# Attention with a relative bias and a three-way maxout layer: reordering the first batches' loads, sums and left-over scores

## The chip, the cores and the metric

The kernel runs on one core of one Trainium2 chip. A core has TensorE (PE in the profile; its weight loads are shown as PEld), VectorE (DVE), ScalarE (ACT), GpSimd (POOL) and SyncE (SP). DMA transfers are issued from the queues of SP, ACT and POOL. The metric is the device time of one execution in microseconds, lower is better. Chances and verdicts are about the median of several executions.

## What is computed

Eight batches of attention with eight heads of 64 columns over 576 positions, and on its result a layer that takes the maximum of three products and multiplies it by a fourth matrix. The reference, cut to what matters:

```python
scores = scale * np.matmul(q, k.transpose(0, 1, 3, 2))      # batch 8, heads 8, seq 576, head_dim 64
bucket = np.where(is_small, n, large)                       # n = abs(row - column)
scores = scores + bias_table[bucket].transpose(2, 0, 1)[None, :, :, :]
attn = np.exp(scores)                                       # after the row maximum is taken off
attn = attn / (np.sum(attn, axis=-1, keepdims=True) + 1e-09)
x = np.matmul(attn, v)                                      # then laid out as 4608 x 512
h = np.maximum(np.maximum(x @ w1, x @ w2), x @ w3)          # 512 x 768 each
out = h @ w_out                                             # 768 x 512
```

## The kernel before

**Tiling.** Batches are counted b = 0 to 7 here, as in the code; the words "batch one" and "batch two" in the change's name are b = 0 and b = 1. Heads go in pairs, hp = 0 to 3. The 576 positions are four tiles of 128 and a left-over of 64. Scores are made transposed (keys on partitions, queries along the free dimension), so that the sums over keys are matmuls with the exponentials as weights. The bias becomes a factor: exponentials near the diagonal are multiplied on VectorE by `hank`, a table of exp(bias), which is what `times_band`, `bands`, `times_bandt` and `times_band_left` do.

**A pair's work.** `visit(qT, kT, e4, c)` (L554) makes the scores of one half of the queries (256) against the four key tiles, as two PSUM tiles `sc` of two banks each, and ScalarE turns each into exponentials in `e4`. `left_keys` (L573) makes the scores of the 64 left-over keys (`sct`), `left_queries` or the optional start of `visit` (L556) those of the 64 left-over queries (`scq`); both write `el`. `attend(b, hp, e4, el, half)` (L604) makes the weighted sums with `v` (`vx` for the four tiles, `vt` for the left-over keys) of one half, in a PSUM tile `a`, and hands back `quotients`, which divides on VectorE. Sums are put off by one pair in the list `late`, and `next_late` (L670) takes the next.

**PSUM.** Three pools of two tiles each: `ps_s` (`sc`, `sct`, the `tp` of b = 1, and `scq` where `left_queries` makes it), `ps_a` (sums, `scq` where `visit` makes it, and a product's first factor while `idle_sums` is not empty), `ps_f` (products `ps`, outputs `pso`, the small transposes). A tile is given out again only when the engine that reads it is done.

**The first batch** (b = 0) has two passes over the pairs, since its inputs arrive piecewise. The first pass visits the first half of the queries; the second (L758 to L810) visits the second half, makes the left-over scores and the sums of half 0, and ends with parts of the first product block. `bands(hp)` multiplies the first half's exponentials.

**Later batches** (L813 to L894) visit both halves of a pair in turn. `together` (L818) says whether the left-over queries are made in `visit` and the half-1 sums follow the left-over keys; it is true from the second pair of b = 2 on. Between the visits `fill(target, hooks)` (L439) puts in portions of the maxout layer up to the target (`rate`) in a count where a product's first, second or third factor counts 4 and an output 6. Hooks run ahead of the last factor or output put in; with three or more of these, a first hook of two runs one place earlier. `add_ffn` cuts a block of tokens into portions; the first 512 tokens come as two blocks of 256 columns (`per` = 2), so that a factor is eight matmuls of 256 columns.

**Queues.** Each engine works in program order. q, k and v are cast to bf16 during their loads, all issued by POOL. The loads of v for b = 0 come between those of q's rest and w_bf[0]; behind them in POOL's queue are b = 1's q and k, the other weights and later batches. SP issues the crossbar transposes of b = 2 and later (L464), those of the attention's result (L651), and the stores. For b = 1 q and k are transposed on TensorE: `second_transposes` (L507), copied out of PSUM by VectorE (`qT`) and ScalarE (`kT`); `spread_packed` (L210) rearranges its loads before that.

The loop's order in b = 1, per pair: visit 0, half-0 sums of the pair before, band 0, quotients, spread of the next pair's q and k, fill with `keys`, visit 1, half-1 sums, band 1, quotients, transposes of the next pair, fill with band 2, left-over queries and band 3.

Of the kernel before, what the change touches and what calls it, by code (L numbers as in the profile page):

```python
# [39 lines left out]
def kernel(  # L40
# [12 lines left out]
    nc = tc.nc  # L53
    B, H, S, D = q.shape
# [78 lines left out]
    def in_turn(b, load):  # L133
        return inorder(load)
# [48 lines left out]
    def load_v(b, h0, h1, behind=None):  # L183
        loads = load_main(v, b, h0, h1, vx[b % 2][:, :, :, 0:D])
        go_behind(loads + load_tail(v, b, h0, h1, v_diag), behind)
# [77 lines left out]
    load_tail(k, 0, 0, H, k_diag)  # L263
    load_main(q, 0, 0, H, batch[0][0], 2, KT)
    load_q_tail(0)
    load_v(0, 0, H)

    def cast_keys(hp):
        h = slice(2 * hp, 2 * hp + 2)
# [38 lines left out]
    def make_bandt():  # L308
        for par in range(2):
            r = slice(64 * par, 64 * par + 64)  # L310
            c = BAND // 2 - 64 * par
            dve_copy(bandt[r, :, :], hank[r, par::2, c : c + 192][:, :, ::-1])
# [4 lines left out]
    def ffn(t0, nt, last):  # L317
# [79 lines left out]
        if per == 1:  # L397
            portions = [[f[0], m[0]]]
            for fb in range(1, n_fb):
                portions.append([g[fb - 1], f[fb], m[fb]])  # L400
            portions.append([g[-1], (0, None), o[0]])
        else:
            if not t0:
                portions = [[f[0]], [m[0], f[1]], [m[1]], [f[2], m[2]]]
                deferred.append(([[g[0]], g[1:]], [[x] for x in o]))
                o = []
            else:
                portions = [x for gs, _ in deferred for x in gs]
                for fb in range(n_fb):
                    portions += [[f[fb], m[fb]], [g[fb]]]  # L410
                portions += [x for _, os in deferred for x in os] + [[o[0]]]
                o = o[1:]
        if len(o) > 2:
# [256 lines left out]
    def next_late():  # L670
        return late.pop(0)() if late else (lambda: None)
# [43 lines left out]
    def bands(hp):  # L715
        for t in range(KT):
            times_band(hp, first_e[hp], t, 0, QS, inorder)
# [40 lines left out]
    for hp in range(HP):  # L758
        qT, kT = (x[:, hp, :] for x in qk[0])
        e4, el = e_tiles()  # L760
        visit(qT, kT, e4, 1, (lambda: more_transposes(hp + 1)) if hp + 1 < HP else None)
        if hp == 0:
            bands(HP - 2)
            bands(HP - 1)

        def keys():
            left_keys(hp, qT, kT, el, QS, S)

        def queries():
            left_queries(hp, qT, kT, el)  # L770

        def late_bands():
            for t in range(KT):
                times_band(hp, e4, t, QS, QM, inorder)

        if hp == 0:
            keys()
            queries()
        if hp == 1:
            x_transposes(0, 0)  # L780
        quotients = next_late()
        if hp < 2:
            quotients()
            if hp == 1:
                keys()
                queries()
                x_transposes(1, 0)
            quotients = next_late()
            quotients()
            if hp == 0:  # L790
                make_bandt()
            late_bands()
            products(hp, el)
        else:
            keys()
            quotients()
            queries()
            late_bands()
            if hp == 2:
                x_transposes(2, 0)  # L800
                x_transposes(3, 0)
                add_ffn(0, QS)
                fill(8)
            else:
                batch[2] = load_tiles()
                load_qk(2)
                x_transposes(0, 1)
                fill(8, lambda: second_transposes(qk[1], 0))
            products(hp, el)
        late.append(lambda hp=hp, e4=e4, el=el: attend(0, hp, e4, el, 1))  # L810

    turned = [lambda hp=hp: x_transposes(hp, 1) for hp in range(1, HP)]
    for b, hp in [(b, hp) for b in range(1, B) for hp in range(HP)]:  # L813
# [1 line left out]
            x_sb[b] = x_tile()  # L815
        qT, kT = (x[:, hp, :] for x in qk[b])
        e4, el = e_tiles()
        together = b > 1 and (b, hp) != (2, 0)  # L818
        rate = 8 if b == 1 or (b, hp) == (2, 0) else 13


# [21 lines left out]

        def keys():
            left_keys(hp, qT, kT, el, 0, S)
            if together:
                next_late()()

        fill(rate, keys, *([lambda: None] if together else []))
        times_bandt(hp, el)  # L850


        visit(qT, kT, e4, 1, el=el if together else None)
        store_outputs()
        if b == 1 or hp in (1, 2) and b + 1 < B:
            next(crossbar, None)
        early()
        if turned:
            turned.pop(0)()
        if not together:  # L860
            quotients = next_late()
            times_band(hp, e4, 1, 0, QM, inorder)
            quotients()
        if b == 1 and hp + 1 < HP:
            second_transposes(qk[1], hp + 1)
        if hp == 1 and b > 1:
            add_ffn((b - 1) * CH, CH)
        if hp == (2, 2, 0)[min(b, 3) - 1] and b + 1 < B:
# [8 lines left out]
            load_qk(b + 2, turned_qk[b + 1, 1, KT - 1])  # L877

        def queries():
            if not together:  # L880
                left_queries(hp, qT, kT, el)
            times_band(hp, e4, 3, 0, QM, inorder)

        def bands_2():
            for t in range(1 if together else 2, 3):
                times_band(hp, e4, t, 0, QM, inorder)

        if together:
            idle_sums.append(hp)
        fill(rate, bands_2, queries)  # L890
        idle_sums.clear()
        times_band_left(hp, el)
        for half in range(2):
# [45 lines left out]
```

The softmax here doesn't subtract the row's maximum and nothing guards it: scores larger than these inputs give would overflow.

## Time and profile before

| | us |
|---|---|
| median of 4 runs (lowest to highest) | 321.02 (320.26 to 321.56) |
| the profiled execution | 322.56 |
| its span, first to last instruction | 320.80 |

| stretch of the span | what runs | us | PE busy | DVE busy | ACT busy | granted clock |
|---|---|---|---|---|---|---|
| 0 to 16 | loads, b = 0 first pass | 16.0 | 11.94 | 8.67 | 11.17 | 1.00 |
| 16 to 36 | b = 0 second pass | 20.0 | 15.88 | 14.64 | 14.10 | 0.83 |
| 63.8 to 76.9 | b = 2, pairs 0 and 1 | 13.1 | 12.89 | 9.43 | 9.81 | 1.00 |
| 76.9 to 98 | b = 2, pairs 2 and 3, start of b = 3 | 21.1 | 19.38 | 15.34 | 14.94 | 1.00 |
| 98 to 262 | the other batches | 164.0 | 162.46 | 114.81 | 115.42 | 1.00 |
| 262 to 320.8 | rest of the maxout layer | 58.8 | 54.84 | 29.06 | 10.98 | 1.00 |

The stretch from 36 to 63.8 is b = 1. The profile is of one execution of the program. Busy times are the union of an engine's instructions in a stretch; matmuls are pipelined and their ends modelled, so a short wait between two of them can hide in a busy figure. The granted clock is the share of full clock that TensorE was given. Idle time ahead of an instruction is shown in brackets with the operation that released it. What starts a wait matters more than the share: an engine that is always busy next to one that sometimes waits sets the pace.

### The profile page before, as it was taken

The numbers are of one execution on the slowest core, as the hardware profiler recorded it, in microseconds if no ns is written. First come the engines' busy times: TensorE is split into PE (matmuls) and PEld (weight loads), VectorE is DVE, ScalarE is ACT, GpSimd is POOL, SyncE is SP. The second block draws the span as 40 slices with busy tenths as digits, with TensorE's granted clock in tenths as the row PEclk, the third lists the DMA queues.
The fourth block names the chain that finished last, engine by engine and source line by source line (L and its number), as shares of the span: only waits on it lengthen the run. The fifth ranks groups of instructions, "written<-read, shape, count | busy, mean of one in ns | idle before, by whom it ended". The sixth has DMA issues, their size and how long they took to land.

```text
span 320.8 us, 8198 instructions
## 1 busy us (share of the span) xinstructions
PE 304.6 (95%) x3288; PEld 172.1 (54%) x3328; DVE 213.6 (67%) x535; ACT 201.2 (63%) x297; POOL 108.2 (34%) x143
## 2 busy tenths in 40 slices
PE   7768899999998999999999999999999999999995
PEld 2356677775554555555555555555555554444442
DVE  6386778786675666667777677776777675554452
ACT  4958898896776667776777677767775751121221
POOL 8938831348049611950294039400000000000000
PEclk9969999999999999999999999999999999999999
DMA  9999999999999999999999959994042103301103
GB/s 167 196 197 198 182 144 135 129 110 141 181 162 155 135 210 141 125 131 181 158 140 143 190 112 153 137 187 108 2 77 98 36 2 74 133 0 67 66 0 131
DMA packets 163878, 40.34 MB, mean 126 GB/s; under 512 B 153720, under 2 KB 159360, under 8 KB 163840
## 3 DMA queue, kind: packets, MB, share of 16 engines
q0 software_dynamic: 103776, 16.66, 78.5%
q1 hardware_dynamic: 58304, 22.69, 38.3%
q10 hardware_dynamic: 1760, 0.47, 0.7%
q8 instruction: 26, 0.43, 0.6%
q14 instruction: 12, 0.10, 0.1%
HBM read 35.39 MB, written 9.45 MB: 140 GB/s over the span
## 4 chain that ended last, share of the span: by engine, by line
PE 69%; DMA 3%; SPq 1%; DVE 1%; issue 1%; ACT 1%
PE ps L94 37%; PE pso L94 13%; PE a L94 11%; PE sc L94 6%; DMA kT<-ktail 2%; PE sct L94 2%; PE scq L94 1%; SPq L464 1%; DMA out_dram<-osb 1%; DVE e L533 0%; ACT e L539 0%; DVE hT L360 0%; DVE m L354 0%; ACT osb L388 0%; SPq L389 0%
## 5 line engine op out<-in xcount | busy, mean ns | idle before, releaser
L94 PE MATMUL ps<-xT,w_bf 128*128 128x512 bf16 (+1 forms) x693 | 148.7, 357 | 2.0 <-ACT xT L107 0.6
L539 ACT ACTIVATE e<-sc 128x1024 bf16<-128x1024 f32 x128 | 124.3, 1030 | 20.5 <-PE sc L94 17.9
L94 PEld LDWEIGHTS <-w_bf 128*128 128x128 bf16 x720 | 65.4, 98 | 63.4 <-issue 5.8
L533 DVE TENSOR_TENSOR e<-e,hank 128x512 bf16<-128x512 bf16 (+2 forms) x136 | 58.6, 467 | 11.7 <-ACT e L539 9.4
L345 ACT ACTIVATE m<-ps 128x512 bf16<-128x512 f32 x48 | 29.2, 608 | 51.9 <-PE ps L94 51.9
L354 DVE TENSOR_TENSOR m<-ps,m 128x512 bf16<-128x512 f32 x48 | 33.1, 689 | 34.1 <-PE ps L94 34.0
L94 PEld LDWEIGHTS <-kT 64*128 64x128 bf16 (+1 forms) x832 | 30.0, 95 | 39.5 <-issue 25.1
L94 PE MATMUL pso<-wo_bf,hT 128*128 128x512 bf16 (+2 forms) x209 | 47.8, 373 | 0.8 <-issue 0.2
L94 PE MATMUL a<-vx,e 128*128 128x65 bf16 x1024 | 46.4, 195 | 0.0
L360 DVE TENSOR_TENSOR hT<-ps,m 128x512 bf16<-128x512 f32 x48 | 33.1, 689 | 15.9 <-PE ps L94 14.4
L94 PE MATMUL sc<-qT,kT 64*128 64x256 bf16 x512 | 41.0, 273 | 2.8 <-ACT e L539 1.8
L94 PEld LDWEIGHTS <-e 128*128 128x128 bf16 x1024 | 42.1, 99 | 0.8
L167 POOL DMA_DIRECT2D q_sb<-in_q_dram x24 | 21.9, 914 | 49.9 <-issue 18.0
L94 PE MATMUL a<-vt,el 128*128 128x130 bf16 x160 | 36.0, 225 | 1.1 <-DMA vt<-in_v_dram 1.1
L139 POOL DMA_DIRECT2D vx<-in_v_dram x32 | 28.4, 912 | 24.4 <-PE sc L94 13.2
L110 DVE COPY osb<-pso 128x512 f32<-128x512 f32 (+1 forms) x33 | 22.6, 686 | 17.9 <-PE pso L94 14.7
L641 DVE TENSOR_TENSOR x_sb<-a,rd 128x256 bf16<-128x256 f32 (+1 forms) x64 | 31.4, 491 | 2.2
L539 ACT ACTIVATE el<-scq 128x256 bf16<-128x256 f32 (+1 forms) x55 | 20.5, 416 | 19.3 <-PE scq L94 19.2
L94 PEld LDWEIGHTS <-hT 128*128 128x128 bf16 x222 | 20.1, 97 | 22.4 <-issue 1.5
L94 PEld LDWEIGHTS <-el 128*128 128x128 bf16 x416 | 24.3, 97 | 10.5 <-issue 5.7
L539 ACT ACTIVATE el<-sct 128x576 bf16<-128x576 f32 (+2 forms) x36 | 21.7, 607 | 7.1 <-PE sct L94 5.8
L167 POOL DMA_DIRECT2D k_sb<-in_k_dram x24 | 22.0, 916 | 1.3 <-DMA w_bf<-in_moe_w_dram 1.2
(71 smaller groups left out, 168.5 us busy)
## 6 DMA issues: line engine op xcount, KB each, us to landing
out_dram<-osb SPq DMA_DIRECT2D x35, 256.0 KB, 2.7
vx<-in_v_dram POOLq DMA_DIRECT2D x32, 128.0 KB, 7.5
q_sb<-in_q_dram POOLq DMA_DIRECT2D x26, 128.0 KB, 5.0
k_sb<-in_k_dram POOLq DMA_DIRECT2D x24, 128.0 KB, 5.6
w_bf<-in_moe_w_dram POOLq DMA_DIRECT2D x3, 768.0 KB, 9.8
xT<-in_k_dram SPq DMA_DIRECT2D x6, 128.0 KB, 4.4
hank<-w_dr SPq DMA_DIRECT2D x2, 384.0 KB, 6.5
wo_bf<-in_moe_w_out_dram POOLq DMA_DIRECT2D x1, 768.0 KB, 8.0
```

The source lines that it names most:

```text
L94: inorder(nc.tensor.matmul(*args, **kw))
L110: return inorder(nc.vector.tensor_copy(out_, in_))
L139: in_turn(b, nc.gpsimd.dma_start(out=dst[:, t, h0:h1, :], in_=x[:, t, h0:h1, :])) for t in range(t0, t1)
L167: loads.append(in_turn(b, nc.gpsimd.dma_start(out=dst[:, t], in_=main_part(src, b)[:, t])))
L345: nc.scalar.activation(out=st[fb]["m0"][:], in_=ps0, func=ACTF.Copy)
L354: inorder(nc.vector.tensor_tensor(out=m[:], in0=ps1, in1=st[fb]["m0"][:], op=ALU.max))
L360: inorder(nc.vector.tensor_tensor(out=block(fb), in0=ps2, in1=other, op=ALU.max))
L464: turned_qk[b, j, t] = inorder(nc.sync.dma_start_transpose(out=made[j][:, :, P * t : P * t + n], in_=src))
L533: put(nc.vector.tensor_tensor(out=e4[:, t, :, lo:hi], in0=e4[:, t, :, lo:hi], in1=hank[:, 2 * hp : 2 * hp + 2, c0:c1][:, :, ::-1], op=ALU. ...
L539: nc.scalar.activation(out=out_, in_=in_, func=ACTF.Exp, scale=inv_sqrt_d)
L641: divided[b, hp, half] = inorder(nc.vector.tensor_tensor(out=x_sb[b][:, 2 * half : 2 * half + n, P * hp : P * hp + P].rearrange("p t (h d) ...
```

## The change

For b = 0, the left-over part of v is loaded ahead of the rest, and the rest head by head (eight loads of four tiles) instead of tile by tile (four loads of eight heads). In the second pass the sums of pair 0 come before its left-over queries, the first half's bands of pair 2 go behind the first sums' quotients and those of pair 3 behind the second ones. In pair 1 the left-over keys and queries go behind the first sums' quotients.

From b = 1 on every pair works as `together` said: left-over queries at the start of the second visit, half-1 sums behind the left-over keys in the first fill, bands 1 and 2 as a hook of the second fill. `second_transposes` becomes a hook of the second fill, between bands and band 3. The portions of the second block of 256 tokens are cut as [first], [second, third] instead of [first, second], [third]. The first fill of pair 1 of b = 2 has the rate 8 instead of 13.

```diff
@@ loads of b = 0
-    load_v(0, 0, H)
+    load_tail(v, 0, 0, H, v_diag)
+    for h in range(H):
+        in_turn(0, nc.gpsimd.dma_start(out=vx[0][:, :, h, 0:D], in_=main_part(v, 0)[:, :, h, :]))
@@ ffn, second block of 256
                 for fb in range(n_fb):
-                    portions += [[f[fb], m[fb]], [g[fb]]]
+                    portions += [[f[fb]], [m[fb], g[fb]]]
@@ second pass of b = 0
         visit(qT, kT, e4, 1, (lambda: more_transposes(hp + 1)) if hp + 1 < HP else None)
-        if hp == 0:
-            bands(HP - 2)
-            bands(HP - 1)
...
         if hp == 0:
             keys()
-            queries()
         if hp == 1:
             x_transposes(0, 0)
         quotients = next_late()
         if hp < 2:
             quotients()
+            if hp == 0:
+                bands(2)
+            else:
+                keys()
+            queries()
             if hp == 1:
-                keys()
-                queries()
                 x_transposes(1, 0)
             quotients = next_late()
             quotients()
             if hp == 0:
+                bands(3)
                 make_bandt()
@@ b = 1 to 7
-        together = b > 1 and (b, hp) != (2, 0)
...
         def keys():
             left_keys(hp, qT, kT, el, 0, S)
-            if together:
-                next_late()()
-
-        fill(rate, keys, *([lambda: None] if together else []))
+            next_late()()
+
+        fill(8 if (b, hp) == (2, 1) else rate, keys, lambda: None)
         times_bandt(hp, el)
...
-        visit(qT, kT, e4, 1, el=el if together else None)
+        visit(qT, kT, e4, 1, el=el)
...
-        if not together:
-            quotients = next_late()
-            times_band(hp, e4, 1, 0, QM, inorder)
-            quotients()
-        if b == 1 and hp + 1 < HP:
-            second_transposes(qk[1], hp + 1)
...
         def queries():
-            if not together:
-                left_queries(hp, qT, kT, el)
             times_band(hp, e4, 3, 0, QM, inorder)
 
         def bands_2():
-            for t in range(1 if together else 2, 3):
+            for t in range(1, 3):
                 times_band(hp, e4, t, 0, QM, inorder)
 
-        if together:
-            idle_sums.append(hp)
-        fill(rate, bands_2, queries)
+        idle_sums.append(hp)
+        turn = [lambda: second_transposes(qk[1], hp + 1)] if b == 1 and hp + 1 < HP else []
+        fill(rate, bands_2, *turn, queries)
```

## The prediction

> **What bounds the kernel now.** I read the page first, then the stretches of the span one by one, then the order of instructions in time where the diff touches. TensorE is busy 304.6 of 320.8 us, so a change pays only where TensorE waits or runs slowly, and costs wherever it makes TensorE wait. Busy shares by stretch, with columns us, PE, PEld, DVE, ACT, POOL busy (instructions), granted clock, DMA share, GB/s:
>
> ```profile
> 4.80:8.20 3.40, 2.29 (x23) 1.15 (x23) 2.48 (x9) 1.82 (x4) 3.40 (x6) 1.00 1.66 207
> ...
> 15.00:18.40 3.40, 1.53 (x20) 0.73 (x16) 2.07 (x7) 3.35 (x6) 0.87 (x3) 1.00 1.66 220
> 18.40:21.80 3.40, 2.50 (x40) 2.35 (x40) 2.53 (x9) 0.43 (x1) 2.76 (x4) 0.51 1.20 207
> 21.80:25.20 3.40, 3.40 (x41) 2.06 (x38) 3.15 (x12) 2.56 (x4) 1.10 (x2) 0.50 1.55 191
> ```
> ```profile
> 36.00:63.80 27.80, 27.16 (x429) 20.96 (x428) 21.63 (x61) 24.73 (x38) 10.31 (x13) 1.00 1.62 145
> ```
> The opening (b = 0, second pass over the head pairs, from 14.9 us) has slack: TensorE is idle for half of 15.0 to 18.4, and runs at half clock for the next 6.8 us. The stretch of b = 1 (36.0 to 63.8) has none: TensorE 98%, and ScalarE, just behind, 89%. The order in time shows what the opening waits for, and a pair of b = 1:
>
> ```profile
> 16.99 0.30 PE L94 MATMUL sct<-qT,kT 128*128 128x320 bf16 x1 [0.80 <-ACT e L539]
> ...
> 17.90 0.29 PE L94 MATMUL scq<-qT,kT 64*128 64x64 bf16 x8 [0.62 <-ACT e L539]
> ...
> 19.30 0.29 PE L94 MATMUL a<-vt,el 128*128 128x130 bf16 x1 [1.10 <-DMA vt<-in_v_dram]
> ```
> ```profile
> 50.93 0.61 PE L94 MATMUL sc<-qT,kT 64*128 64x256 bf16 x8
> ...
> 51.41 1.94 ACT L539 ACTIVATE e<-sc 128x1024 bf16<-128x1024 f32 x2 [0.76 <-PE sc L94]
> ...
> 52.08 1.03 PE L94 MATMUL ps<-xT,w_bf 128*128 128x256 bf16 x8
> ...
> 52.95 0.41 PE L94 MATMUL sct<-qT,kT 128*128 128x512 bf16 x2
> ...
> 54.16 0.66 PE L94 MATMUL sc<-qT,kT 64*128 64x256 bf16 x8
> ...
> 54.60 1.94 ACT L539 ACTIVATE e<-sc 128x1024 bf16<-128x1024 f32 x2 [0.22 <-PE sc L94]
> ...
> 56.83 0.78 DVE L110 COPY qT<-tp 128x512 bf16<-128x512 bf16 x2
> ...
> 57.79 0.61 PE L94 MATMUL sc<-qT,kT 64*128 64x256 bf16 x8
> ```
> Pair 2 of b = 1 takes 6.86 us (50.93 to 57.79). The product at 52.08 stands between the sums and the left-over keys (sct), so the first exponential has ended before sct needs its PSUM buffer, and the second visit's exponentials start at 54.60, 3.67 us after the pair's start. One more row, at b = 3: TensorE waits 1.15 us for the transposed left-over keys, at full load otherwise:
>
> ```profile
> 97.93 0.42 PE L94 MATMUL sct<-qT,kT 128*128 128x512 bf16 x2 [1.15 <-DMA kT<-ktail]
> ```
>
> **Part 1, the opening: −2.1 us.** Now the sums of pair 0 wait for all of v, tail last (issued 11.66 to 12.95, landing 7.0 to 7.4 us later, 19.2). Changed, the two tail loads go first (1.29 us of POOL for both) and eight head loads follow. A head is 64 KB; qtail, 64 KB, took 0.69 us to issue, vx, 128 KB, 0.88. So eight take 5.5 to 7.0 us against 3.52, and w_bf[0] behind them is issued 2.0 to 3.5 us later than 12.89. It landed at 23.5 and is first read at 29.67, which covers that. Heads 0 and 1 are issued by about 11 us. Loads issued at 8.2 and 9.1 landed 4.2 us later, at 13.3 the latest; the one issued at 9.95, beside the hank loads, 8.1 later. So they land between 14.5 and 18.5; I take 15 to 16, since less is queued ahead of them. Then the sums of pair 0 start behind sct at 17.2 instead of 19.30 (bands of pair 0 end at 17.0), left-over queries follow at 17.9 as now, sums of pair 1 at 18.2, and the scores of pair 1 at 18.7 instead of 21.60.
>
> Those 2.9 us don't all last: DVE is late next. From 18.1 its queue holds quotients 0.55, bands 0.92, quotients 0.55, bands 0.92, two bandt copies 0.71, late bands 0.88, products 0.30 and the qT copy 0.32, together 5.15 (each from its row's start to the next start): 23.3. TensorE then still has 0.12 of transposes (they wait for that copy's PSUM) and 0.60 of sums before pair 2's scores: 24.0 against 26.00 now. From there both orders are the same. I take −2.1, between −0.2 (heads at 19) and −2.9.
>
> Two rules of the Trainium skill against rows. "TensorE: Matmul & The Clock Gate", section "Why this matters for your kernels", asks for no idle gap over about 3 us to keep full clock. The longest wait here is 1.10 us, and still the clock halved at 18.4: what decides is the busy share of a stretch, lost with 1.53 of 3.40 us, kept with 2.29. By the rule the changed opening can't be throttled and all of −2.1 stands. By the rows 15.0 to 18.4 gets 0.6 of sums more and about 0.2 of left-over queries (2.3, just enough), but 21.8 to 25.2 now holds the DVE wait and about 1.9 of work: if that halves the clock for 6.8 us, pairs 2 and 3 lose 1.5 and −0.6 is left. I take the rule's side for the value and the rows for the range. "DMA: Bandwidth & Descriptors", section "Anatomy of one DMA — SWDGE (gpsimd) path", prices a load at 2.0 us plus bytes over 436 GB/s: eight times 2.15 against four times 2.3, if they were serial, is 8 us later, and pair 3's heads (due at 23.5) would be missed. But four loads issued within 3.5 us were in flight together here, so only issue time counts; I take the rows.
>
> **Part 2, b = 1 and pair 0 of b = 2: +4.8 us.** Left-over queries move into the second visit, the half-1 sums into the first fill behind sct, the transposes of the next pair behind bands 1 and 2, and per first fill there is one product of eight matmuls instead of up to two. Nothing is removed but one exponential of 0.60, which becomes two (0.66). So little can be won: TensorE has 0.64 us idle in all of 36.0 to 63.8. What is lost is in the chain. Pair 2, from its first score matmul at 0:
> - first exponential 0.48 to 1.48 (51.41 and 0.97 each); sct has no product ahead of it now, waits for that PSUM buffer and starts at 1.55 (pair 1 shows it now: 43.62, sct at 45.17);
> - half-1 sums 1.80 to 2.70, product to 3.65, its copy on ScalarE 3.9 to 4.4;
> - behind it on ScalarE the two left-over exponentials, 0.55: the second visit's exponentials start at 4.95 instead of 3.67 and end at 6.9. ScalarE stood idle 0.6 to 1.0 of that, waiting for the product;
> - TensorE: left-over queries wait for the quotients (3.8), scores to 4.5, product to 5.45, then the transposes wait for the exponential at 6.0;
> - DVE: bands 1 and 2 stand ahead of the qT copy now, band 2 needs the last exponential: 7.35, the copy 0.78, and pair 3's scores start at 8.2. TensorE idles before them by 0.6.
> 8.2 against 6.86 is +1.35. The same table for the others: pair 0 +1.45 (six-wide quotients 0.70 twice and spread copies 0.93 hold the left-over queries until 4.4), pair 1 +0.85 (an xT copy of 0.36 on ScalarE in place of the product's), pair 3 +0.5 and pair 0 of b = 2 +0.8 (no transposes; second scores and next sums wait for the last exponential and band 2), pair 1 of b = 2 −0.15 (its products, 12 then 6, become 6 then 12, which covers waits of 0.41 and 0.47 at 77). Sum 4.8. The table put to the present order gives 63.4 and 94.7 for rows at 63.83 and 94.60, so I trust it to about 1 us. Bounds: +0.3 (five times 0.06 of ScalarE) and +5.5.
>
> **Part 3, the 1.15 us at 97.93: −1.2 us.** Batch 3's q and k loads wait on POOL until the last quotients of b = 1 (issued at 70.11, 4.09 after the tail before them), and SP's transposes follow. Those quotients now belong to the first fill of that pair, about 2.4 us earlier relative to TensorE, so the chain gains on TensorE by more than 1.2. POOL and SP have nothing else queued there. Bounds 0 and −1.5. The other DMA edge, batch 2's left-over keys (landing 62.3, read at 65.9), is safe while Part 2 delays TensorE.
>
> **Sum.** −2.1 + 4.8 − 1.2 = +1.5 on the profiled execution's 322.56 (span 320.80 and 1.76 around it): 324.1. The median of the runs, 321.02, lies 1.54 below that execution, so the forecast is 322.5.
>
> **Rivals.** Faster: the chain of b = 1 closes without waits because TensorE's products cover it, and only +0.3 remains: −2.1 − 1.2 + 0.3 = −3.0, 318.0. For it: ScalarE and DVE have 3 and 6 us free there, and later batches run this very order at 99%. Against: they have 12 or more 512-wide matmuls per fill to hide behind, b = 1 has 8 or 16 of 256. It is decided where Part 2 costs less than 3.3. Slower still: the heads arrive in the hank loads' shadow (the 8.1 us row) or the clock stays halved, Part 1 gives −0.2: +3.4, 324.4. Level: the three terms cancel, because Part 2 is half my size: 321.0, or the moved steps don't meet the path.
>
> **Chances.** Forecast (322.5, own range 320.6 to 324.5) 0.55; faster rival 0.22; slower still 0.15; level 0.08. About 0.3% (1 us) can be told from no change. Faster takes 0.19 of the rival and 0.02 of the forecast's tail: 0.21. Same takes level, 0.08 of the forecast and 0.03 of the rival: 0.19. Slower 0.60. The range 318.5 to 325.4 holds the forecast, the slower case and half of the faster one.
>
> **What would show it.** Sums of pair 0 at 17 to 17.5 and scores of pair 2 near 24; clock 1.00 from 18 to 32. In b = 1, sct waiting for the exponential, transposes waiting for PSUM and scores waiting for the qT copy, and 8 us from pair to pair; the wait at the later sct gone. If TensorE stays at 97% from 34 to 62 us, Part 2 is wrong and the kernel is faster.

## The result, and the profile after

The changed kernel takes 322.44 us in the median of 35 runs (321.18 to 323.98), against 321.02 for the kernel before in the same job (54 runs). The ratio is 1.0044, 95% interval 1.0032 to 1.0057: slower by 1.4 us. 322.5 was forecast. Ratios here and below are formed from fast executions, those within 1.5% of the fastest of their kernel, and are not the quotients of the medians, which count all.

| | before | after |
|---|---|---|
| profiled execution, us | 322.56 | 322.50 |
| its span, us | 320.80 | 320.70 |
| start of pair 0's left-over keys (`sct`), second pass of b = 0 | 16.99 | 18.12 |
| start of b = 1 | 36.04 | 34.37 |
| start of pair 3 of b = 2 | 86.27 | 87.52 |
| left-over keys of b = 3 | 97.93 | 97.87 |

The two profiled executions are the same length, while the medians are 1.4 us apart: the profiled execution of before was a poor one of its kind, 1.5 us above its median, and that of after is an ordinary one. Comparing the two traces alone would have said "no change". The first pass of b = 0 took 1.13 us longer in the profile of after, so its left-over keys start later although b = 1 starts earlier.

Busy time by stretch in the profile of after, with the columns us, then PE, PEld, DVE, ACT and POOL busy (instructions), granted clock, DMA share and GB/s:

```profile
15.00:18.40 3.40, 2.15 (x26) 1.20 (x23) 2.30 (x8) 3.40 (x6) 2.39 (x4) 1.00 2.06 180
18.40:21.80 3.40, 3.38 (x77) 2.59 (x74) 2.68 (x10) 2.91 (x5) 3.40 (x6) 1.00 1.17 205
21.80:25.20 3.40, 2.19 (x41) 1.48 (x41) 3.29 (x13) 2.41 (x6) 1.15 (x2) 1.00 1.57 189
...
36.00:63.80 27.80, 24.48 (x386) 19.11 (x383) 20.33 (x55) 21.59 (x38) 10.83 (x15) 1.00 1.71 149
```

The opening keeps the full clock from 15 to 25.2, where before had 0.50 for 6.8 us. From 36 to 63.8, nearly all of it b = 1, TensorE falls from 27.16 to 24.48 us busy, and ScalarE and DVE fall with it: no engine is busy nearly all the time now, they wait for each other. The order in time (start, duration, engine, line, operation, idle time before it with its releaser) shows how:

```profile
18.12 0.30 PE L94 MATMUL sct<-qT,kT 128*128 128x320 bf16 x1 [0.80 <-ACT e L541]
18.25 0.22 PE L94 MATMUL a<-vt,el 128*128 128x130 bf16 x1
...
23.89 0.32 DVE L110 COPY qT<-tp 128x320 bf16<-128x320 bf16 x1
...
24.26 0.39 PE L94 MATMUL sc<-qT,kT 64*128 64x256 bf16 x4 [0.73 <-DVE qT L110]
...
50.70 0.61 PE L94 MATMUL sc<-qT,kT 64*128 64x256 bf16 x8 [0.52 <-DVE qT L110]
...
52.25 0.41 PE L94 MATMUL sct<-qT,kT 128*128 128x512 bf16 x2 [0.24 <-ACT e L541]
...
53.39 1.04 PE L94 MATMUL ps<-xT,w_bf 128*128 128x256 bf16 x8
...
54.97 0.66 ACT L541 ACTIVATE el<-scq 128x256 bf16<-128x256 f32 x2
...
55.51 1.95 ACT L541 ACTIVATE e<-sc 128x1024 bf16<-128x1024 f32 x2
...
56.60 0.38 PE L97 MATMUL tp<-ident,q_sb 128*128 128x128 bf16 x4 [0.23 <-ACT e L541]
...
57.09 1.02 DVE L535 TENSOR_TENSOR e<-e,hank 128x768 bf16<-128x768 bf16 x2
...
58.02 0.78 DVE L110 COPY qT<-tp 128x512 bf16<-128x512 bf16 x2
...
58.76 0.61 PE L94 MATMUL sc<-qT,kT 64*128 64x256 bf16 x8 [0.57 <-DVE qT L110]
...
63.16 1.92 PE L94 MATMUL ps<-xT,w_bf 128*128 128x256 bf16 x16
...
65.56 0.39 PE L94 MATMUL sc<-qT,kT 64*128 64x256 bf16 x4 [0.16 <-ACT e L541]
...
97.87 0.41 PE L94 MATMUL sct<-qT,kT 128*128 128x512 bf16 x2
```

Sums of pair 0 now follow the left-over keys at once (18.25), and the longest wait behind them is for DVE's qT copy (24.26), as forecast. Pair 2 of b = 1 runs from 50.70 to 58.76, 8.06 us against 6.86: `sct` waits for the exponential, the second visit's exponentials start 4.81 us in instead of 3.67, the transposes 5.90 in, and the qT copy comes behind the bands. At b = 3 the wait of 1.15 us is gone.

Pair by pair from the start of b = 1 (us from each pair's first score matmul to the next pair's):

| | (1,0) | (1,1) | (1,2) | (1,3) | (2,0) | (2,1) | (2,2) | sum |
|---|---|---|---|---|---|---|---|---|
| before | 7.58 | 7.31 | 6.86 | 6.04 | 6.04 | 7.05 | 9.35 | 50.23 |
| after | 8.54 | 7.79 | 8.06 | 6.25 | 6.30 | 7.45 | 8.76 | 53.15 |
| difference | +0.96 | +0.48 | +1.20 | +0.21 | +0.26 | +0.40 | −0.59 | +2.92 |

In these two traces b = 1 starts 1.67 earlier, its pairs and those of b = 2 cost 2.92, and from the start of b = 3 to its left-over keys 3.33 becomes 2.01: −1.67 + 2.92 − 1.32 = −0.07, which is the −0.06 between the two executions. What a typical execution does needed the experiments.

### The profile page after: what moved, and what is told of

Same layout as the page of the kernel before. It is cut to its first block, busy times and chain, and to the rows that moved or that the text cites. A ratio compares the mean times of both kernels' runs of the same rounds, so it can differ in the third digit from the quotient of the medians.

```text
span 320.7 us, 8208 instructions
## 1 busy us (share of the span) xinstructions
PE 303.9 (95%) x3288; PEld 171.7 (54%) x3328; DVE 213.5 (67%) x535; ACT 201.5 (63%) x302; POOL 110.9 (35%) x147
## 4 chain that ended last, share of the span: by engine, by line
PE 79%; ACT 2%; DVE 2%; issue 2%; DMA 1%; DVEq 0%
PE ps L94 41%; PE pso L94 14%; PE a L94 13%; PE sc L94 8%; PE sct L94 2%; PE scq L94 2%; ACT e L541 2%; DVE e L535 1%; DMA out_dram<-osb 1%; DVE x_sb L643 0%; DVE hT L353 0%; DVE hT L362 0%; ACT kT L107 0%; ACT osb L390 0%; DVE k_sb L213 0%
## 5 line engine op out<-in xcount | busy, mean ns | idle before, releaser
L535 DVE TENSOR_TENSOR e<-e,hank 128x512 bf16<-128x512 bf16 (+2 forms) x136 | 59.4, 472 | 8.6 <-ACT e L541 8.4
L94 PE MATMUL a<-vx,e 128*128 128x65 bf16 x1024 | 45.0, 193 | 0.0
L94 PEld LDWEIGHTS <-e 128*128 128x128 bf16 x1024 | 40.7, 97 | 0.9
L139 POOL DMA_DIRECT2D vx<-in_v_dram x28 | 24.8, 900 | 29.0 <-PE scq L94 15.0
```

What stands on the lines that cost most here:

```text
L94: inorder(nc.tensor.matmul(*args, **kw))
L139: in_turn(b, nc.gpsimd.dma_start(out=dst[:, t, h0:h1, :], in_=x[:, t, h0:h1, :])) for t in range(t0, t1)
L535: put(nc.vector.tensor_tensor(out=e4[:, t, :, lo:hi], in0=e4[:, t, :, lo:hi], in1=hank[:, 2 * hp : 2 * hp + 2, c0:c1][:, :, ::-1], op=ALU. ...
```

## The experiments

All were timed beside the kernel before, whose median differs from job to job: 321.02 for the first four below, 320.75 for the next four, 321.17 for the next three and 320.62 for the last. So medians of different jobs can be told apart only roughly; the ratio is to the kernel before in the same job. The start of b = 1 and the time from pair 0's left-over keys to it are collected in one table behind them.

**The kernel before, once more.**

> The kernel before, unchanged, run as a kernel of its own, so that the clock of each of its executions is listed. The two profiled spans are equal (320.8 and 320.7) while the medians differ by 1.4, so the profiled execution of before is not a typical one. Theory 1: it lost more clock than most (0.989, 6.8 us at half clock behind 18.4); typical executions have 0.995 to 1.000 and a span near 319.3. Theory 2: the clock has nothing to do with it; spans vary by 1 to 2 us at equal clocks, and a second profile has its own waits in the opening. Ratio 1.000 by both.

Measured: 321.01 us (22 runs), ratio 1.0004 (0.9987 to 1.0021); profiled execution 321.95. Stretches of 2 us of this profile, columns as above:

```profile
8.00:10.00 2.00, 1.71 (x15) 0.79 (x11) 0.87 (x3) 1.89 (x2) 2.00 (x4) 1.00 2.03 180
...
18.00:20.00 2.00, 0.58 (x12) 0.35 (x11) 1.86 (x8) 2.00 (x3) 1.16 (x2) 1.00 1.19 210
20.00:22.00 2.00, 2.00 (x37) 2.00 (x35) 1.14 (x4) 0.62 (x2) 1.03 (x2) 0.50 1.24 206
```

The clock halves here too, two us later and for a shorter time than in the first profile: the second pass takes 17.21 us instead of 19.05. But this execution was slow earlier. Until about 13 us its matmuls take as long as at half clock, although the stretches give 1.00 there; four score matmuls of the first pass, here and in the first profile of before:

```profile
9.81 0.61 PE L94 MATMUL sc<-qT,kT 64*128 64x256 bf16 x4 [0.29 <-DVE kT L110]
```
```profile
8.28 0.39 PE L94 MATMUL sc<-qT,kT 64*128 64x256 bf16 x4 [0.51 <-ACT e L539]
```

So pair 0's left-over keys start at 18.83 instead of 16.99, and b = 1 starts at 36.04 in both profiles. The wait at b = 3's left-over keys is 0.54 instead of 1.15, and these 0.61 us are the whole difference of the two spans (320.18 and 320.79). Theory 1's span near 319.3 didn't come. By the start of b = 1 the first profile had lost no more than this one; only its DMA wait was longer.

**The opening alone** (loads of v and order of the second pass, nothing from b = 1 on).

```diff
-    load_v(0, 0, H)
+    load_tail(v, 0, 0, H, v_diag)
+    for h in range(H):
+        in_turn(0, nc.gpsimd.dma_start(out=vx[0][:, :, h, 0:D], in_=main_part(v, 0)[:, :, h, :]))
...
             quotients()
+            if hp == 0:
+                bands(2)
```

> Before with the opening alone changed (v's tail first, v head by head, sums ahead of left-over queries, bands of pairs 2 and 3 later). Theory 1 (a path of waits): b = 1's first scores come 2.1 to 2.8 us earlier than in a profile of before with the same clock in the first pass; ratio 0.991 to 0.995. Theory 2 (the gain is only the clock of one odd execution): ordinary executions of before don't lose clock there, and the gain is under 0.7 us, ratio 0.998 or more. If the parts add, this ratio times that of the later part alone gives 1.0044.

Measured: 320.90 us (23 runs, 319.12 to 326.67), ratio 0.9983 (0.9965 to 1.0001), hardly a gain: by this interval the opening is worth 0 to 1.1 us, by its middle 0.5. The profiled execution is a long one, 325.49. b = 1 starts at 33.18, 2.86 before the old one, but b = 2 shows a wait that the prediction did not list. POOL's row and TensorE's, in order of time:

```profile
61.56 3.52 POOL L139 DMA_DIRECT2D vx<-in_v_dram  x4 [8.15 <-PE sc L94]
...
72.43 0.27 PE L94 MATMUL a<-vt,el 128*128 128x130 bf16 x1 [4.80 <-DMA vt<-in_v_dram]
72.49 0.65 PE L94 MATMUL a<-vx,e 128*128 128x65 bf16 x8
```

The sums of (2,0) wait 4.80 us for batch 2's v. POOL issues that load behind the fourth key tile that SP has turned for b = 2, a chain of DMAs that didn't move when TensorE was earlier (61.26 in the trace of before with b = 1 at 36.04, 61.56 here with b = 1 at 33.18). And its landing is uneven: the left-over part took 6.6 to 6.9 us here, 3.1 to 3.5 in the profile of after. Behind the wait eight sums take 0.65 us instead of 0.41: the clock has gone too.

**Everything from b = 1 on, the opening left as before.**

```diff
-                    portions += [[f[fb], m[fb]], [g[fb]]]
+                    portions += [[f[fb]], [m[fb], g[fb]]]
...
-        together = b > 1 and (b, hp) != (2, 0)
...
+        turn = [lambda: second_transposes(qk[1], hp + 1)] if b == 1 and hp + 1 < HP else []
+        fill(rate, bands_2, *turn, queries)
```

> Before with everything from b = 1 on changed and the opening left alone. Theory 1 (the chain through ScalarE and VectorE): the pairs from b = 1 pair 0 to b = 2 pair 2 take 2.9 us longer together, as in the profile of the changed kernel, and the wait of 1.15 us at b = 3's left-over keys goes: +1.7, ratio 1.0055. Theory 2 (the wait doesn't go when this part stands alone, because TensorE is late by less than the loads gain): +2.9, ratio 1.009. Theory 3 (most of the 1.4 us comes from the opening): ratio below 1.002.

Measured: 322.88 us (7 runs), ratio 1.0064 (1.0039 to 1.0089): 1.9 to 2.1 us slower. This is Parts 2 and 3 of the prediction together. By the median it is more than the whole change costs, though the intervals overlap; 0.9983 for the opening times 1.0064 is 1.0047, near the 1.0044 of both, so the parts add. The pairs are those of the changed kernel (8.52, 7.79, 7.99, 6.25, 6.31, 7.44), and `sct` of b = 3 doesn't wait. The surprise is in the opening, in the old order:

```profile
17.60 0.30 PE L94 MATMUL sct<-qT,kT 128*128 128x320 bf16 x1 [0.80 <-ACT e L539]
...
18.74 0.23 PE L94 MATMUL a<-vt,el 128*128 128x130 bf16 x1
...
20.04 0.39 PE L94 MATMUL sc<-qT,kT 64*128 64x256 bf16 x4
...
23.30 0.32 DVE L110 COPY qT<-tp 128x320 bf16<-128x320 bf16 x1
...
23.67 0.39 PE L94 MATMUL sc<-qT,kT 64*128 64x256 bf16 x4
```

This execution lost no clock from 16 to 36 us. v was there when the sums of pair 0 came, pair 2's scores start 6.07 us behind pair 0's left-over keys (6.14 in the changed kernel), and b = 1 starts 16.12 behind them (16.25 in the changed one). In both, pair 2's scores come when DVE's qT copy is done (the rows at 23.30 here and 23.89 there), and it starts 5.70 and 5.77 us behind the left-over keys. At full clock the old order is as quick as the new one.

**The q and k loads of b = 3 earlier, else as before.**

```diff
-            load_qk(3, divided[1, HP - 1, 1])
+            load_qk(3, divided[1, HP - 1, 0])
```

> Before with one word changed: batch 3's q and k loads go behind the quotients of half 0 of b = 1's last pair (66.3 in the profile of before) instead of half 1 (69.8). Theory 1 (the wait at 97.93 hangs on when these loads start): POOL issues them from about 67, SP's transposes begin up to 3 us earlier unless SP's own five transposes of the attention result hold them, and the wait of 1.15 us goes: -1.2, ratio 0.996. Theory 2 (SP's transposes are held by the half-1 result, which they stand behind in SP's order, or by the rate of the transposes): the wait stays, ratio 0.999 to 1.000.

Measured: 320.93 us (22 runs), ratio 1.0001 (0.9986 to 1.0016). The wait at b = 3's left-over keys is gone from the profile, whose span is 0.7 us shorter than that of before once more, and the median doesn't move. By itself the 1.15 us that Part 3 counted is worth nothing that these runs can tell.

**The opening with batch 2's v earlier.**

```diff
-            load_v(b + 1, 0, H, turned_qk[b + 1, 1, KT - 1] if b < 3 else None)
+            load_v(b + 1, 0, H, turned_qk[b + 1, 1, KT - 1 if b > 1 else 1] if b < 3 else None)
```

> The opening alone, and batch 2's v issued by POOL behind the second key tile of batch 2 turned by SP instead of the fourth, some 5 us earlier (before it was issued at 61.3 to 66.0 and landed at 69.5). Theory: the opening starts b = 1 about 2.5 us earlier, and what took the gain in the opening alone was this load, which follows SP's transposes and not TensorE (a wait of 4.80 us of the sums of pair 0 of b = 2). Then the wait is gone, the sums of (2, 0) start at 67.5 to 68, and the median is 318.3 to 319.3, ratio 0.991 to 0.995, with no runs above 323. Rival A: the gain was never there in typical executions (before's own opening does as well where the clock is kept): 320.5 to 321.2. Rival B: the earlier v delays batch 2's last transposes, and the wait moves to the scores or left-over keys of (2, 0): 320 to 323.

Measured: 320.66 us (22 runs, 319.17 to 322.97), ratio 1.0003 (0.9984 to 1.0022). The wait is gone, as is the tail of long runs (none above 322.97; six of 23 were above 324 without the edit). The median is Rival A's, 320.5 to 321.2. But the edit moved the issue and hardly the landing:

```profile
53.62 3.54 POOL L139 DMA_DIRECT2D vx<-in_v_dram  x4
57.09 1.30 POOL L158 DMA_DIRECT2D vt<-in_v_dram  x2
```

The left-over part, last issued at 57.7, took up to 12.0 us and was there at 69.7; in before, last issued at 65.4, it took 3.8 and was there at 69.2. So the sums of (2,0) could hardly start before that here either (they start at 69.83), and this run doesn't show what the opening gives where v comes earlier. In the profile b = 1 starts at 34.90 only, since this execution lost its clock in the first pass (0.50 from 7 to 14 us), which the change doesn't touch; and another DMA edge has come up, b = 2's left-over keys, which the prediction had called safe only while Part 2 delays TensorE:

```profile
65.27 0.42 PE L94 MATMUL sct<-qT,kT 128*128 128x512 bf16 x2 [0.40 <-DMA kT<-ktail]
```

**The same, with b = 3's loads earlier as well** (both edits above on the opening).

> As the kernel before it in this list, and the loads of q and k of b = 3 issued behind the half-0 quotients of b = 1's last pair instead of its half-1 ones. Theory: once TensorE reaches b = 3 earlier, its left-over keys are the next DMA edge (1.15 us waited for in the profile of before, 0.5 in a second one), so this is worth 0.5 to 1.2 us on top: 317.3 to 318.8, no wait at the left-over keys of b = 3. Rival: nothing on top, as in the same edit of the kernel before alone (ratio 1.0001): within 0.3 us of the other.

Measured: 319.87 us (14 runs), ratio 0.9997 (0.9973 to 1.0021), 0.8 below the kernel without the second edit, where 0.5 to 1.2 were expected, but above the 317.3 to 318.8 of the theory, and the interval doesn't exclude no gain over before. Its profile starts the sums of (2,0) at 68.88, just behind batch 2's v (68.7). Here the clock was lost inside the new second pass, 0.58 and 0.57 from 24 to 28, behind a stretch (22 to 24) in which TensorE was busy 1.06 of 2.00 us while it waited for DVE. This is the loss that the prediction priced on its "rows" side.

**The changed kernel, with the transposes ahead of bands 1 and 2.**

```diff
-        fill(rate, bands_2, *turn, queries)
+        fill(rate, *turn, bands_2, queries)
```

> The changed kernel with the transposes of the next pair ahead of bands 1 and 2 in the second fill instead of behind them. Theory: in b = 1 the chain from pair to pair ends with the last exponential, band 2, qT copy, next scores; with the copy no longer behind band 2 a pair with transposes takes 7.4 to 7.8 us instead of 8.06 (pair 2), three pairs together 0.8 to 1.5 us less, median 321.0 to 321.7. Rival: the transposes need PSUM of the score pool, which the last exponential frees, and bands then stand behind the copies and hold the next half-1 sums: the wait moves, the periods stay within 0.2 of 8.5, 7.8, 8.0, median 322.2 to 322.9.

Measured: 321.76 us (10 runs), ratio 1.0065 (1.0032 to 1.0099) to the kernel before. The median is 0.7 below the changed kernel's, the ratio isn't (1.0044 there), so in time these runs show no gain.

```profile
56.02 0.79 DVE L110 COPY qT<-tp 128x512 bf16<-128x512 bf16 x2 [0.18 <-PE tp L97]
...
56.73 1.35 DVE L535 TENSOR_TENSOR e<-e,hank 128x768 bf16<-128x768 bf16 x3
...
56.79 0.61 PE L94 MATMUL sc<-qT,kT 64*128 64x256 bf16 x8
...
72.37 0.23 PE L94 MATMUL a<-vt,el 128*128 128x130 bf16 x1 [2.13 <-DMA vt<-in_v_dram]
```

The copy stands ahead of the bands, and pair 3's scores (56.79) follow without a wait for DVE. The three pairs take 8.07, 7.26 and 7.52 us, together 1.5 less than changed. So in the trace the copy behind band 2 is the end of b = 1's chain, as the prediction had it. In this execution 2.13 us of it are lost again at batch 2's v.

**The kernel before with the new loads of v for b = 0 only.** The diff is the first hunk of the opening.

> The kernel before with the loads of v of b = 0 as changed (left-over part first, then head by head), and nothing else. Theory: the sums of pair 0 lose their wait for v (1.10 us), but they stand behind the left-over queries and bands in the old order, so b = 1 starts 0.5 to 1.2 us earlier than 36.04 at like clock, and the rest of the opening's 2.9 us is the order's: median 320.4 to 321.0. Rival: the loads are all of it: b = 1 at 33.5, and the wait for batch 2's v at (2, 0) shows as in the opening alone; median 320.5 to 321.2 with some runs above 324.

Measured: 320.99 us (22 runs), ratio 0.9997 (0.9976 to 1.0017). b = 1 starts at 35.92, 17.12 us behind pair 0's left-over keys, and the clock is halved from 20 on as in before. The sums of pair 0 don't wait for v, but they didn't in the second profile of before either, whose first pass was as late (18.83; 18.80 here). So v in time doesn't save the clock; what the earlier loads give behind a quick first pass wasn't seen. The wait at b = 3's left-over keys is absent here too (96.50, 2.02 us behind the start of b = 3), though nothing was done to those loads.

**The kernel before with both DMA edges moved** (v of b = 2 and the loads of b = 3), and **the same with two idle matmuls** in pair 0 of the second pass:

```diff
         if hp == 0:
+            keep_warm()
             keys()
+            keep_warm()
             queries()
```

> The kernel before with batch 2's v behind the second key tile of batch 2 and the q and k loads of b = 3 behind the half-0 quotients; opening and pairs of b = 1 as before. A control for the kernel that has these two and the new opening (319.87). Theory: the old opening still loses the clock in the second pass (half clock from about 20 to 23 us, b = 1 at 36.0), TensorE is too late for batch 2's v to matter, and only the 0.5 to 1.2 us at b = 3's left-over keys goes: 320.3 to 321.0 in the median, that is 0.5 to 1 us more than with the new opening. Rival: the two loads alone bring what was measured, and the opening nothing: 319.6 to 320.1.

> As the control, and in pair 0 of the second pass two idle matmuls of 512 columns (zeros, 0.4 us each) in the gaps ahead of the left-over keys and of the left-over queries, where TensorE waits 0.80 and 0.62 us for the exponentials; the order is the old one. Theory: the new order of the opening gains nothing at full clock, because DVE's list up to the qT copy of pair 2 is the same (from pair 0's left-over keys to the start of b = 1: 16.12 us in the old order where the clock was kept, 16.1 to 16.3 in the new one), and all of its gain is the clock. Then 16 to 26 shows clock 1.00, pair 2's scores start 6.0 to 6.2 us behind pair 0's left-over keys, b = 1 starts 16.0 to 16.4 us behind them (17.2 to 19.05 where the clock was lost), and the median is as with the new opening, 319.4 to 320.2. Rival A: the clock follows other things than this busy share and halves again at about 20: b = 1 17 us or more behind, median as the control. Rival B: the clock is kept and still b = 1 starts 17 us or more behind: then the order itself was worth 1 us.

Measured: 320.32 us for the control (22 runs, ratio 0.9980, 0.9959 to 1.0000) and 320.03 for the other (22 runs, 319.13 to 321.10, ratio 0.9966, 0.9948 to 0.9984). The control lies at the lower end of its theory's range. With the new opening in place of the idle matmuls it was 319.87, ratio 0.9997 (in another job). The second of them is the only kernel of this study whose whole interval lies below 1: about 1.1 us faster than before, and 2.4 below the changed kernel's median. Its profile:

```profile
18.00:20.00 2.00, 1.12 (x15) 0.50 (x14) 1.85 (x7) 1.95 (x4) 1.44 (x3) 1.00 1.18 212
20.00:22.00 2.00, 2.00 (x47) 1.50 (x45) 1.66 (x7) 0.96 (x2) 0.75 (x1) 1.00 1.21 205
```

Where the kernel before once more had 0.58 us of work and then half clock, this has 1.12 and full clock, and b = 1 starts 16.00 us behind pair 0's left-over keys, in the old order. That fits the theory's numbers (pair 2's scores 5.95 behind, 6.0 to 6.2 expected). Three profiles of the old order with as slow a first pass (left-over keys at 18.83, 18.69 and 18.80; 18.71 here) all lost the clock at 20. Of the control's 22 runs eight have a mean clock of 0.988 or 0.989, of the other's none is below 0.993. But the two medians are only 0.3 us apart and their intervals overlap; that the idle matmuls are worth something in time isn't shown by these runs.

**The changed kernel with the transposes first and both DMA edges moved.**

> The changed kernel with the transposes of the next pair ahead of bands 1 and 2 (321.76 by itself) and the two earlier loads. Theory: by itself it lost 2.1 us of its gain at the sums of pair 0 of b = 2, which waited for batch 2's v; with v earlier the wait is gone, b = 2's third pair starts 1.5 us or more earlier than in the changed kernel (its left-over keys 79.5 to 80 against 81.20 there, at like clock), and the median is 319.9 to 320.8, below the changed kernel's 322.44 by 1.6 or more. Rival: the other transfers of b = 2 (its left-over keys, landing at about 62.5) or b = 1's exponentials hold it again: 321.2 to 322.

Measured: 321.38 us (14 runs), ratio 1.0004 (0.9983 to 1.0026), 1.06 below the changed kernel's median: the rival's range. Its interval and that of the changed kernel (1.0032 to 1.0057) don't meet, so the two edits together do take time off it. The wait for v is gone. This execution lost its clock at 24 to 28, and the three pairs took 8.41, 7.20 and 7.80; in pair 2 the wait has moved to the left-over queries:

```profile
54.82 0.29 PE L94 MATMUL scq<-qT,kT 64*128 64x64 bf16 x7 [0.49 <-DVE x_sb L643]
```

**The new order only in the pairs without transposes** ((1,3), (2,0), and the rate 8 in (2,1)), old portions:

```diff
-        together = b > 1 and (b, hp) != (2, 0)
+        together = b > 1 or hp == HP - 1
```

> The kernel before, with the new order only in the pairs that have no transposes behind them: the last pair of b = 1, pair 0 of b = 2, and the rate 8 in pair 1 of b = 2. The three pairs of b = 1 with transposes, the portions and the opening stay. Theory: these pairs were priced too high (+0.5, +0.8, -0.15, together +1.15); the changed kernel's profile has them at 6.25, 6.30 and 7.45 us against 6.04, 6.04 and 7.05, and gives 0.59 back in pair 2 of b = 2, because the smaller fill of pair 1 leaves its products where they cover more. Then from the start of b = 1's last pair to the start of b = 2's last pair it is 28.6 to 28.9 us against 28.48 before and 28.76 changed, and the median lies within 0.5 us of before. Rival: with the old portions of two factors a fill, these pairs cost what the prediction said, 29.3 to 29.8 us, median 1 us or more above before.

Measured: 321.85 us (22 runs), ratio 1.0031 (1.0013 to 1.0049). My theory missed and the rival's number came: from pair 3 of b = 1 to pair 3 of b = 2 it is 29.51 us, against 28.48 before and 28.76 changed.

```profile
61.42 1.05 PE L94 MATMUL ps<-xT,w_bf 128*128 128x256 bf16 x8
...
62.70 0.39 PE L94 MATMUL sc<-qT,kT 64*128 64x256 bf16 x4 [0.23 <-ACT e L539]
63.61 0.39 PE L94 MATMUL sc<-qT,kT 64*128 64x256 bf16 x4 [0.52 <-ACT e L539]
```

With the old portions the second fill holds one product (1.05 us), and the next pair's scores wait 0.23 and 0.52 for the second visit's exponentials. In the changed kernel the second fill holds two (the row at 63.16: 16 matmuls, 1.92 us), and the wait is 0.16. So the cut of the portions makes the new order cheap in these pairs: 0.75 us over them. With the old portions (2,0) takes 6.85 us, the +0.8 that was forecast, and (1,3) 6.15.

The second pass of b = 0 in all profiles, from pair 0's left-over keys to the start of b = 1 (us):

| order | clock kept from 16 to 36 | clock lost there |
|---|---|---|
| old | 16.12 (b = 1 on changed), 15.99 (pairs without transposes), 16.00 (idle matmuls) | 19.05 (before), 17.21 (before again), 17.33 (b = 3's loads), 17.12 (loads of v), 18.18 (both edges) |
| new | 16.25 (changed), 16.22 (opening alone), 16.13 (with v), 16.59 (transposes first) | 17.15 (with v and b = 3's loads), 17.83 (transposes first, both edges) |

Counted from the start of the span, which takes in what the first pass lost, b = 1 starts at 35.45 to 36.04 in the five old ones with the clock lost, at 33.72 to 34.81 in the three old ones with it kept, and at 33.18 to 34.90 in the six new ones.

## Why the prediction was right, and where it wasn't

The total was right, +1.4 measured against +1.5, and its direction for the reason that was given: b = 1 costs more than the opening gains. That it came so close is luck: two of its terms were off by about as much in opposite directions.

**Part 1, the opening (−2.1 forecast, about −0.5 measured, 0 to −1.1 by the interval).** −0.5 is the opening alone by its ratio, and −0.44 the difference between the changed kernel and the one with everything from b = 1 on (322.88 to 322.44). With both DMA edges moved, the kernels with the old and the new opening lie 0.85 and 0.88 below before in their own jobs, so nothing can be told there. The failed step is the subtraction "24.0 against 26.00 now". The 26.00 was the old order at half clock. At full clock the old order ends in the same DVE queue at the same time: 6.07 us behind the left-over keys against 6.14. The moved sums and earlier heads gain nothing there.

The 24.0 was met (24.26), but by two errors. DVE's list was worked out correctly: 5.16 us from the first quotient at 19.05 to the end of the copy, against 5.15. The 0.72 us of transposes and sums that were put behind the copy had been done before it (the last sums start at 23.13), so the chain from the left-over keys takes 6.14 us instead of the 7.0 of the forecast; and this execution's left-over keys start 1.13 later than the row that the forecast began at.

What the opening changes is how often the clock is lost: from 16 to 36 us in two of six profiles instead of five of seven without idle matmuls. The clocks of all executions say it more firmly: the mean recorded clock is 0.997 or more in 77 of 118 executions with the new opening, in 38 of 310 with the old one, and in 12 of 22 with the idle matmuls. For the clock the prediction took the side of the Trainium skill's rule ("TensorE: Matmul & The Clock Gate", section "Why this matters for your kernels": no gap over about 3 us, so none lost) and kept "−0.6 is left" for the rows' side. The rows' side came near the size of −0.5, and the loss at about 24 us behind the DVE wait that it described is in two profiles. But a kept clock isn't yet time: at 0.997 or more the opening alone has a median of 320.82 (13 runs), with v earlier 320.57 (18), and the kernel before one of 319.80 (24). Why these executions aren't faster stays open. One limit is batch 2's v: in twelve of the fourteen profiles its last part landed between 67.5 and 69.7 us, whatever TensorE did and however early it was issued, and in the other two at about 72.3.

Of the two prices for the head loads, the rows' one held: POOL issued the eight in 6.06 us, they landed 3.8 to 6.7 us after their issue, so in flight together, and no sums wait for them.

**The DMA edges.** "Safe while Part 2 delays TensorE" was said of batch 2's left-over keys, and holds: in the changed kernel nothing waits there. The nearer edge, batch 2's v, was not listed. It isn't reached in the profile of the changed kernel either, where Part 2 delays TensorE, but it took 4.80 and 2.13 us in the profiles of two versions that are quicker in b = 0 or b = 1. In both the load landed late, at about 72.3.

**Part 2 (+4.8 forecast, +2.9 in the trace).** The chain was right link by link where it was written out: pair 2 had second exponentials at 4.95 (measured 4.81), transposes at 6.0 (5.90), next scores at 8.2 (8.06). The forecasts of +1.45, +0.85 and +1.35 came out as +0.96, +0.48 and +1.20. Moving the transposes and their copy ahead of the bands takes 1.0 to 1.5 us off these three pairs. Of the 1.9 us too much, 1.0 is in these pairs, half of it in pair 0: its left-over queries came 4.38 us in, as forecast (4.4), and what follows took less; which step is not worked out here. The other 0.9 is in the pairs without transposes: (1,3) +0.5 and (2,0) +0.8 measured +0.21 and +0.26, for (2,0) because two products in the fill ahead of it cover the exponentials; the prediction had read the new portions as a cost only. Pair (2,1) was −0.15 and came out +0.40, and (2,2), which wasn't priced, gives 0.59 back.

**Part 3 (−1.2 forecast).** The wait went, in the changed kernel and in every version that moved these loads or had the new order. In the two traces it is worth −1.32. In medians it is nothing by itself; Parts 2 and 3 together are +1.9 to +2.1 against 2.92 − 1.32 = +1.6 from the two traces. That the removal alone doesn't show in the median fits a wait that differs from execution to execution: with these loads and the order as before it was 1.15, 0.54 and, in the kernel with the new loads of v only, nothing. How it is spread over the unprofiled executions isn't shown.

**The base.** The sum was set on one profiled execution and shifted by 1.54 to the median. 0.61 of the 1.54 is its longer wait at b = 3, against the second profile of before, and Part 3 counted the whole wait as a gain once more. Its halved clock doesn't explain the rest: b = 1 starts at 36.04 in both profiles, and at 36.02 and 35.92 in two more of the old order whose times, 321.25 and 321.14, are near the medians. What the other 0.9 us are stays open.

## What to carry to other kernels

Before counting a wait or a slow stretch of the profile as a gain, profile the unchanged kernel again: what an execution lost by chance (here the place of the halved clock and half of a DMA wait) isn't the change's to win. Compare the end of a chain at the same clock in both orders, and also from the start of the span, since a stage can look shorter only because the one before it was longer. When a part of the kernel is made earlier, go down the list of every transfer due in the next stages that isn't paced by the engine you speed up, and read off its margin. Check the landing and not the issue: here a load that was issued 7.6 us earlier landed no earlier. Where left-over work moves between two fills, look which fill keeps the products that cover the long exponentials: cutting the products differently was worth 0.75 us here.

## What the runs showed of the hardware

The clock was halved for one stretch in most profiles, each time for 3.4 or 6.8 us (the last two microseconds of the span left out), in differing places: 18 to 25 us (before), 20 to 23 (before again), 7 to 14 (the opening with v), 24 to 28 (with b = 3's loads). In four profiles of the old order matmuls take as long as at half clock from 5 to 13 us, without a recorded half clock (the rows at 9.81 and 8.28 above), so a mean recorded clock can leave out what an execution lost at its start. The busy share ahead of the loss doesn't settle it alone. In the kernel with the new order only in pairs without transposes TensorE had the same 0.58 us of work from 18 to 20 as in the second profile of before, and the clock stayed whole:

```profile
18.00:20.00 2.00, 0.58 (x11) 0.35 (x11) 2.00 (x9) 2.00 (x3) 1.37 (x3) 1.00 1.25 210
20.00:22.00 2.00, 2.00 (x49) 1.60 (x47) 1.43 (x7) 0.92 (x3) 0.99 (x2) 1.00 1.20 205
```

That execution had lost its clock earlier, from 7 to 14 us, as had the profile of after (11 to 14.3) and that of the opening with v, both of which kept it in the second pass. An earlier slow stretch doesn't always protect: in three of the four profiles with slow matmuls up to 13 us the clock was lost again at 20, and the fourth is the one with the idle matmuls. A lost stretch in the second pass goes with 1 to 3 us more from the left-over keys to b = 1 (the table above). In the kernel before, the time goes with the recorded clock in part: of 193 runs in four jobs, the 22 with a mean of 1.000 have a median of 319.56, the 120 with 0.995 one of 321.01, but the 13 with 0.989 one of 320.36. The changed kernel's 35 runs show no such relation (322.61 for the 8 at 1.000, 321.96 for the 16 at 0.999, 322.38 for the 6 at 0.995); that it waits for ScalarE and DVE instead would fit, and isn't shown. And a wait of 2.13 us for a DMA was followed by half-speed matmuls (from 73.6 us in the version with the transposes first: 0.65 us for eight sums that take 0.41).
